# Q tiles scaled once and placed by small DMAs, sums normalised in their own buffers, a longer planned latency: a two-layer attention and MLP kernel on one core

## The chip, the core and the metric

The kernel runs on one core of one Trainium2 chip. Five engines of that core work side by side, each on its own queue of instructions and in the order of that queue: TensorE (PE, matrix products, written to PSUM), VectorE (DVE), ScalarE (ACT), GpSimd (POOL) and SyncE (SP). Here SP only starts DMA transfers, which sixteen DMA engines then carry out, and POOL starts some too. Engines wait for one another, and for DMAs, through semaphores. The metric is the device time of one execution in microseconds; a lower number is better.

## The reference

Two layers share their weights. Each layer is a self-attention block with 32 heads of 16 features and an MLP block with a ReLU. Both add to the residual stream `x` of 2048 rows and 512 columns (bf16), and both normalise their input without learned gains.

```python
def _A_ref(x, wqkv, wo):
    qkv = transpose((x @ wqkv).reshape(B, S, 3, H, Dh), 2, 0, 3, 1, 4)
    q, k, v = qkv[0], qkv[1], qkv[2]
    scores = einsum("bhqd,bhkd->bhqk", q, k) * (Dh ** -0.5)
    p = softmax(scores, axis=-1)
    o = einsum("bhqk,bhkd->bhqd", p, v)
    return transpose(o, 0, 2, 1, 3).reshape(B, S, D) @ wo
def _B_ref(x, w1, w2):
    return relu(x @ w1) @ w2

x = x + _A_ref(_layernorm(x), A_wqkv, A_wo)
x = x + _B_ref(_layernorm(x), B_w1, B_w2)
x = x + _A_ref(_layernorm(x), A_wqkv, A_wo)
x = x + _B_ref(_layernorm(x), B_w1, B_w2)
```

The costly part is the exponential: 32 heads x 2048 x 2048 scores in each layer.

## The kernel before

**Tiles.** The 2048 query rows are cut into chunks of 512 (the last two chunks of layer 1 are cut in halves of 256). A chunk is worked through in runs. A run is one T of four; T names 128 features of Q and K, that is eight heads. Within a T, a head is found by its group g (32 partitions each, four of them) and its parity e (which 16 of the 32). A run has two segments, one for each parity. A segment goes over blocks: 128 keys by 512 queries of one head.

**Slots.** The main loop forms slots of three blocks (W = 3). For each block PE makes the scores in one of two PSUM tiles `ps_s` of three banks (L1396), with a contraction over 32 partitions: 16 of the head and 16 of its neighbour, which must be zero in Q. ACT takes the exponential of the slot, out to `e` (L1405). In about half of the slots the third block goes to DVE instead, which makes its exponential from integer and half-precision steps on pairs of such blocks (`lin` L1090, then `step` and `cube` from L1131 on). ACT's instruction has then 1024 columns instead of 1536. PE multiplies the exponentials with the values, adding up in `ps_o` (L983). The values carry a column of ones, so that the sum of the exponentials comes out in a row of its own.

**Q.** `q_group` (L682) makes the Q tile of one run with sixteen matmuls into `ps_f` (L446). Its end, `fin`, lets DVE multiply the bank with two columns of a mask (L676): one read per parity, both written to `qbuf[n % 2]`, with the scale in the mask and zeros where the other parity stands. So DVE reads the bank twice in one instruction. The group for run n + 1 is put on the urgent list as soon as a block of run n is first taken.

**The end of a segment.** `finish_segment` (L867) copies `ps_o` to one of three buffers `u`, or, for segments whose first part was summed up earlier, adds the stored part to it and writes to `u` (L895, L897). SP then moves the row of sums to a compact tile `c` (L902), DVE takes the reciprocal (L924), SP puts it back (L925), and POOL spreads it over 32 partitions to one of three buffers `r` by a DMA (L927). For "quick" segments a DVE shuffle does the spreading instead (L937). At last DVE multiplies `u` with `r` into `ot` (L913), from which the output projection is made. A new segment's copy waits, through `run_until(("m", n - NU))`, until the product three segments earlier has been put in order.

**The rest.** Projections, layer norms and the MLP (`o_group`, `h_group`, `z_group`, K and V groups) are cut into pieces that fill PE between the slots. Weights of the MLP's first half come in tiles of 128 columns into four buffers `w1buf`; the load of tile n + 4 is issued by SP behind the matmuls of tile n (L714). Normalised rows are transposed by DMA from SP too (L571).

**What sets the order.** The order of instructions on each engine is written out by a planner that runs when the kernel is built. It keeps a clock for PE, DVE and ACT with fixed costs, marks when each result will be there (`mark`, with a planned lag for what comes by DMA: C_LAG for `c`, R_LAG for `r` by POOL, U_LAG for the quick ones), and puts an instruction in its queue when its inputs are due. On the chip nothing but the queues' order and the semaphores counts. One rule matters below: when the planner looks for a block for DVE, it may take one of a later run (FAR = 3 segments ahead), if that run's Q is marked at all:

```python
sg["l"] == mine["l"] and ahead.count(sg) + (sg is mine) > 1
and at([("q", sg["n"])], "pe") is not None
```

The pace of the filling work is `todo` divided by the slots that are left in the chunk, less or plus a constant.

Of the kernel before, what the change touches and what calls it, by code (L numbers as in the profile page):

```python
# [12 lines left out]
BF16 = mybir.dt.bfloat16  # L13
# [4 lines left out]
ALU = mybir.AluOpType  # L18
# [7 lines left out]
def kernel(  # L26
# [10 lines left out]
    nc = tc.nc  # L37
    P = 128
# [5 lines left out]
    DH = D // H  # L44
# [6 lines left out]
    QS = 512  # L51
    NQS = S // QS
    TPC = QS // P
    NT = 8
    SCALE = float(DH) ** -0.5
# [2 lines left out]
    NE = 5  # L58

    NACC = 8  # L60
    NW1 = 4
    NU = 3


# [2 lines left out]
    LOG2E = 1.4426950408889634  # L67
    UNIT = 128.0
# [8 lines left out]
    PE_TO_DVE, DVE_TO_PE, ACT_TO_PE, PE_TO_ACT = 220.0, 180.0, 240.0, 222.0  # L77
    DVE_TO_DVE, EVAC = 112.0, 612.0
    FLOOR = 0.56
    C_LAG, R_LAG, U_LAG = 3600.0, 10500.0, 3000.0  # L80
    VLAG = 1
    X_ISSUE, X_LAG = 1400.0, 7500.0
    RSTD_LAG = 4000.0
    AHEAD = (8.0, 8.0)
    LATE = 0.0
    MID = 2
# [15 lines left out]
    def sb(shape, dt, name):  # L102
        return persist.tile(shape, dt, name=name)
# [6 lines left out]
    wo = sb([P, NDC, D], BF16, "wo")  # L110
    w1buf = [sb([P, NDC, P], BF16, f"w1_{n}") for n in range(NW1)]
    w2 = sb([P, NF, D], BF16, "w2")
# [38 lines left out]
    acc0.append(kt1[:].bitcast(FP32).rearrange("p a b -> p (a b)"))  # L151
    ebuf = [sb([P, W * QS], BF16, f"e{n}") for n in range(NE)]
    qbuf = [sb([P, 2, QS], BF16, f"q{n}") for n in range(2)]
    ubuf = [sb([P, QS], FP32, f"u{n}") for n in range(NU)]
    rbuf = [sb([P, QS], FP32, f"r{n}") for n in range(NU)]
    cbuf = [sb([P, QS // 32], FP32, f"c{n}") for n in range(NU)]
# [38 lines left out]
    nc.sync.dma_start(out=w2[:], in_=B_w2[:, :].rearrange("(c p) f -> p c f", p=P))  # L195

    make_identity(nc, ident[:])
    for kb in range(NKB):
        nc.gpsimd.memset(vaug[0][kb][:, :, DH : DH + 2], 1.0)
    for kb in range(NKB - TPC):  # L200
# [47 lines left out]
    def mark(key, engine="dve", lag=0.0):  # L248
        made[key] = (engine, (now_pe if engine == "pe" else now_dve)[0] + lag)
# [135 lines left out]
    def finish_group():  # L385
        while cur:
            do_piece()
        while evac:
            do_evac()

    def run_until(key):

        if key in made:
            return
        finish_group()
        if key in made:
            return
        if key not in maker:
            kind, l, j = key[1]
            for i in range(chunks[l, j][1]):  # L400
                run_until(("z", l - 1, j, i) if kind == "ln1" else ("o", l, j, i))
        if key in made:
            return
        t = maker[key]
        for k in t["deps"]:
            run_until(k)
        if "pieces" in t:
            start_group(t)
            finish_group()
        else:  # L410
            do_task(t)
        assert key in made, key
# [51 lines left out]
    LAST = 5  # L464

    def columns(l, j):

        tt, n = chunks[l, j]
        return tt // TPC, tt % TPC * P, n * P
# [78 lines left out]
    def ln_rows(tag, tt, n, i):  # L548
# [10 lines left out]
        if i == n - 1:  # L559

            def rstd():
                ln_seed(tag, n)
                mark(("rs", tag, 3), lag=RSTD_LAG)

# [54 lines left out]
    def each(n, *key):  # L619
        return [key + (i,) for i in range(n)]  # L620
# [54 lines left out]
    def q_masked(n, b, w=QS):  # L675
        return nc.vector.tensor_mul(  # L676
            out=qbuf[n % 2][:, :, 0:w],
            in0=b.rearrange("p (e q) -> p e q", e=1).to_broadcast((P, 2, w)),
            in1=qmask.rearrange("p (e q) -> p e q", q=1).to_broadcast((P, 2, w)),
        )  # L680

    def q_group(n, l, j, T):  # L682
        xj, _, w = columns(l, j)
        cost = 90 + 2.09 * w

        def fin(b):
            q_masked(n, b, w)
            mark(("q", n))

        return mm_group(  # L690
            q_mms(l, j, T), fin, [("q", n)], each(TPC, "xnT", ("ln1", l, xj)), cost=cost,
            wide_by=w,
        )
# [16 lines left out]
    def load_w1(n):  # L710

        if n < len(chunks) * NF - NF + NW1:
            ft = n % NF
            nc.sync.dma_start(  # L714
                out=w1buf[n % NW1][:],
                in_=B_w1[:, ft * P : (ft + 1) * P].rearrange("(c p) f -> p c f", p=P),
# [5 lines left out]
    def h_group(l, j, ft, war):  # L722
# [19 lines left out]
        def after():  # L742
            for f in range(number):
                load_w1(n + f + NW1)
            if w1_to_load:
# [7 lines left out]
            [  # L753
                (w1buf[(n + f) % NW1][:, c, :], xnT[xj][:, c, a : a + w])
                for f in range(number) for c in range(NDC)
# [39 lines left out]
    def rest_of_chunk(l, j):  # L795

        if (l, j) == (1, LAST - 2):
            for ft in range(NF):
                home = (
                    w1buf[((l * NQS + LAST) * NF + ft) % NW1] if ft < NW1  # L800
                    else (kt01 + kt2)[(ft - NW1) // 2][:, ft % 2, :].rearrange(
# [61 lines left out]
    last_steps = []  # L863

    sums_wait = [0]

    def finish_segment(sg, last):  # L867
        l, j, t, e = sg["l"], sg["j"], sg["t"], sg["e"]
# [13 lines left out]
        n = norm_no[0]  # L882
        norm_no[0] += 1
        if n >= NU:
            run_until(("m", n - NU))
        u, r, c = ubuf[n % NU], rbuf[n % NU], cbuf[n % NU]
        lane = DH if e == 0 else DH - 1
        width = sg["w"]
        at_column = columns(l, j)[1]
# [1 line left out]
        c = c[:, 0 : width // 32]  # L891
# [17 lines left out]
        b = before(l, j)  # L909
# [258 lines left out]
    for e in range(2):  # L1168
        nc.vector.tensor_reduce(
            out=mask[e],  # L1170
            in_=ident[:].rearrange("p (g e d) -> p e g d", g=4, e=2)[:, e],
# [3 lines left out]
            out=qmask[:, e : e + 1], in0=mask[e], scalar1=SCALE * LOG2E * UNIT, scalar2=None,  # L1175
            op0=ALU.mult,
# [24 lines left out]
    b = plain(k_mms(0, 0))  # L1201
# [6 lines left out]
    b = plain(v_mms(0))  # L1208
# [58 lines left out]
    while units:  # L1267
# [6 lines left out]
        for (sg, kb, g), *_ in banked:  # L1274
            if sg["n"] not in seen:
                seen.add(sg["n"])
                n = sg["n"] + 1
# [12 lines left out]
        if len(banked) == W and pair_at in (None, no):  # L1290
# [3 lines left out]
            elif (not pairs or pair_no[0] + 1 - pairs[0]["n"] < NP) and ((mine['l'] or ("v", 0, 15) in made or len(pairs) < 3 and ("v", 0, 5) in made or not pairs and ("k", 0, 0, 1) in made) and (not mine['l'] or ('k', 1, 0, NQS - 1) in made or pace < PAIR_PACE)):  # L1294
# [7 lines left out]
                if now_dve[0] + waiting < now_pe[0] + BACKLOG:  # L1302
                    here = segs.index(mine)
                    first = max(here, segs.index(pairs[-1]["sg"])) if pairs else here
# [10 lines left out]
            if half is not None:  # L1315
# [22 lines left out]
                if far:  # L1338
                    units.remove(far)
                    units.appendleft(banked.pop())  # L1340
                    x = far
                elif fit or of_take:
                    x = fit or next((x for x in of_take[::-1] if x[0][2] not in other), of_take[-1])
                    banked.remove(x)
                else:
                    units.appendleft(banked.pop())
                    x = take_unit(heads(banked) + other, take)
# [13 lines left out]
        todo = left()  # L1361
        first = now[0][0]
        rest = to_come[first["l"], first["j"]] / W
        if first["l"] and first["early"]:
            rest = sum(x[0][0]["early"] for x in itertools.islice(units, 400)) / W - 20.0
        pace = (
            3.0 if first["short"] and not first["l"] else max(todo / max(rest + (-8.0 if first["j"] == NQS - 1 and not first["l"] else AHEAD[first["l"]] if first["j"] < (LAST if first["l"] else NQS - 1) else -6.0), 6.0), 0.5)
        )
        owed[0] = min(owed[0] + pace, 6.0) if todo else 0.0
        hurry[0] = pace > (  # L1370
# [15 lines left out]
        short = FLOOR * 1330.0 - level - busy[0] - MM * (1 + soon)  # L1386
        times = 1 + min(spare, max(0, math.ceil(short / MM)))
        b = ps_s[no % 2][:].rearrange("p w q -> p (w q)")
# [13 lines left out]
        m = len(now) - len(taken)  # L1402
        while len(pend) == NE:
            force_v()
        ex = nc.scalar.activation(  # L1405
            out=eb[:, 0 : place[m]], in_=b[:, 0 : place[m]], func=ACTF.Exp,
# [33 lines left out]
    l, j = 1, LAST  # L1440
# [60 lines left out]
    for ft in range(NF + 1):  # L1501
        if ft < NF:
            b = more[ft % 4]
# [5 lines left out]
            if ft % 2:  # L1509
                out = nc.scalar.activation(out=ht[ft][:, at_column : at_column + width], in_=at_bank(b)[:, 0:width], func=ACTF.Relu)  # L1510
            else:
                out = nc.vector.tensor_scalar(
                    out=ht[ft][:, at_column : at_column + width], in0=at_bank(b)[:, 0:width],
                    scalar1=0.0, scalar2=None, op0=ALU.max,
                )
# [7 lines left out]
    for i in rows:  # L1523
# [3 lines left out]
            out=out_flat[(tt + i) * P : (tt + i + 1) * P, :], in_=x_t[tt + i][:]  # L1527
# [31 lines left out]
```

The softmax here doesn't subtract the row's maximum and nothing guards it: scores larger than these inputs give would overflow.

## Time and profile before

| | |
|---|---|
| median of 3 runs | 1589.63 us (1586.18 to 1590.61) |
| the profiled execution | 1588.44 us, of which 1586.6 us from its first to its last instruction |
| TensorE clock granted | 0.995 |
| exponentials on ACT | 1366, of them 702 with 1024 columns |
| Q evacuations on DVE | 52, the first by itself in the start |
| DMAs issued by SP | 353, of them 24 transposes |
| POOL's spreads r<-u | 59; 7.3 us (256 KB) and 4.9 us (128 KB) from issue to landing |

A row of the groups reads: line, engine, operation, what is written and read with shapes, count; then busy time in us and mean duration in ns; then the engine's idle time just before these instructions and what ended most of it. A row of the timeline reads: start and length in us, engine (a q behind it means its queue, which only issues), line, operation, tiles, count, and in brackets the idle time before with its releaser. An instruction's duration contains pipelining with its neighbours: exponentials overlap by some 0.1 to 0.25 us, and DVE instructions by some 0.1.

### The profile page before, as it was taken

The page shows a single profiled execution, that of the slowest core. Times are in us where ns is not written, and L with a number is a line of the kernel's source. Part 1 is how long each engine was busy: PE and PEld are TensorE (multiplying, and loading weights), DVE is VectorE, ACT ScalarE, POOL GpSimd, SP SyncE. Part 2 cuts the span into 40 slices and gives each one's busy share as a digit, 9 for nine tenths or more (in the row PEclk, how much of TensorE's full clock was granted, in tenths as well). Part 3 has the DMA queues.
Part 4 walks back from the last instruction along what each step waited for, and adds up shares of the span by engine and source line. Part 5 has one row for each costly group of instructions (what it writes and reads, how often), then busy time and mean ns, then how long its engine had stood idle before and what let it go on. Part 6 is the DMA issues. An engine that isn't in the chain of part 4 may idle for free.

```text
span 1586.6 us, 45174 instructions
## 1 busy us (share of the span) xinstructions
PE 1430.4 (90%) x19752; PEld 536.9 (34%) x19752; DVE 1506.7 (95%) x2910; ACT 1545.3 (97%) x1383; POOL 101.3 (6%) x240
## 2 busy tenths in 40 slices
PE   8888889998899989999899998888999999999898
PEld 3222223222233322322223222223334444544454
DVE  7899999999999999999899998899999999999994
ACT  7999999999999999999999999999999999999994
POOL 2000001001010010100100001001001000010100
PEclk9999999999999999999999999999999999999998
DMA  6001101111012120120101000000210111313030
GB/s 193 15 2 26 18 9 22 39 25 25 6 19 45 23 29 7 25 48 13 26 2 28 21 2 1 2 4 9 54 25 16 40 33 27 74 26 80 13 62 15
DMA packets 128885, 45.57 MB, mean 29 GB/s; under 512 B 117840, under 2 KB 125776, under 8 KB 128688
## 3 DMA queue, kind: packets, MB, share of 16 engines
q1 hardware_dynamic: 114752, 29.36, 8.6%
q0 software_dynamic: 12592, 12.02, 4.3%
q8 instruction: 154, 2.52, 0.7%
q10 hardware_dynamic: 1344, 1.31, 0.2%
q14 instruction: 43, 0.35, 0.1%
HBM read 24.38 MB, written 2.10 MB: 17 GB/s over the span
## 4 chain that ended last, share of the span: by engine, by line
ACT 81%; PE 8%; DVE 7%; issue 2%; DMA 1%; ACTq 0%; DVEq 0%
ACT e L1405 81%; PE ps_s L1396 3%; PE ps_f L446 2%; DVE lin L1090 2%; PE ps_o L983 2%; DVE step L1131 1%; PE ps_s L1458 1%; DVE cube L1146 1%; DVE cube L1142 1%; DMA wqkv<-in_A_wqkv_dram 1%; DMA r<-u 0%; DVE ht L736 0%; DVE q L676 0%; DVE ot L913 0%; DVE stats L481 0%
## 5 line engine op out<-in xcount | busy, mean ns | idle before, releaser
L1405 ACT ACTIVATE e<-ps_s 128x1536 bf16<-128x1536 f32 (+1 forms) x1366 | 1536.7, 1362 | 8.5 <-PE ps_s L1396 8.1
L1396 PE MATMUL ps_s<-q,ktp 32*128 32x512 bf16 (+1 forms) x6136 | 608.1, 341 | 112.4 <-ACT e L1405 99.2
L983 PE MATMUL ps_o<-e,vaug 128*32 128x512 bf16 (+1 forms) x4236 | 500.8, 346 | 14.1 <-DVE u L897 8.3
L1090 DVE TENSOR_SCALAR lin<-ps_s 128x512 int16<-128x512 f32 x702 | 478.3, 685 | 24.5 <-PE ps_s L1396 18.1
L1396 PEld LDWEIGHTS <-ktp 32*128 32x128 bf16 x6136 | 200.3, 92 | 563.6 <-issue 418.9
L1131 DVE TENSOR_SCALAR step<-lin 128x1024 int16<-128x1024 int16 x702 | 275.3, 419 | 1.9 <-PE ps_o L983 0.9
L983 PEld LDWEIGHTS <-vaug 128*32 128x32 bf16 x6052 | 173.8, 95 | 300.9 <-issue 282.2
L1142 DVE TENSOR_TENSOR cube<-step 128x1024 f16<-128x1024 bf16 x351 | 238.4, 683 | 1.6 <-PE ps_o L983 0.2
L1146 DVE TENSOR_TENSOR cube<-cube,lin 128x1024 bf16<-128x1024 f16 x351 | 238.0, 679 | 0.0
L446 PE MATMUL ps_f<-w,ht 128*32 128x512 bf16 x1624 | 151.6, 381 | 1.8 <-DVE x L768 0.5
L446 PE MATMUL ps_f<-xnT,w 128*32 128x512 bf16 (+1 forms) x2016 | 146.3, 345 | 5.8 <-DVE ht L736 3.6
L983 PE MATMUL ps_o<-step,vaug 128*32 128x512 bf16 (+1 forms) x884 | 151.0, 340 | 0.0
L983 PE MATMUL ps_o<-cube,vthird 128*32 128x512 bf16 (+1 forms) x836 | 148.9, 339 | 0.0
L983 PE MATMUL ps_o<-lin,vaug 128*32 128x512 bf16 (+1 forms) x884 | 125.9, 339 | 4.6 <-DVE u L897 3.2
L927 POOL DMA_DIRECT2D r<-u x59 | 43.1, 731 | 1168.6 <-DVE lin L1090 341.7
L446 PE MATMUL ps_f<-xnT,wqkv 128*32 128x512 bf16 (+1 forms) x1312 | 109.4, 365 | 6.2 <-DVE ktp L626 1.1
L446 PE MATMUL ps_f<-wo,ot 128*32 128x512 bf16 x960 | 90.3, 381 | 1.2 <-DVE x L700 1.2
L736 DVE TENSOR_SCALAR ht<-ps_f 128x512 bf16<-128x512 f32 x105 | 72.0, 685 | 2.3 <-PE ps_f L446 1.5
L446 PEld LDWEIGHTS <-w 128*32 128x32 bf16 x2016 | 57.5, 96 | 33.9 <-issue 18.7
L676 DVE TENSOR_TENSOR q<-ps_f,masks 128x1024 bf16<-128x1024 f32 (+1 forms) x51 | 53.6, 1052 | 9.1 <-PE ps_f L446 8.1
L446 PEld LDWEIGHTS <-ht 128*32 128x32 bf16 x1624 | 46.9, 96 | 25.3 <-issue 11.9
L983 PEld LDWEIGHTS <-vthird 128*32 128x32 bf16 x836 | 43.6, 95 | 33.5 <-issue 28.7
(103 smaller groups left out, 609.4 us busy)
## 6 DMA issues: line engine op xcount, KB each, us to landing
w<-in_B_w_dram SPq DMA_DIRECT2D x130, 128.0 KB
r<-u POOLq DMA_DIRECT2D x32, 256.0 KB, 7.3
r<-u POOLq DMA_DIRECT2D x27, 128.0 KB, 4.9
out_dram<-x SPq DMA_DIRECT2D x16, 128.0 KB
x<-in_A_x_dram SPq DMA_DIRECT2D x14, 128.0 KB
w<-in_B_w_dram SPq DMA_DIRECT2D x1, 1792.0 KB
ktp<-in_B_w_dram SPq DMA_DIRECT2D x10, 128.0 KB
wqkv<-in_A_wqkv_dram ACTq DMA_DIRECT2D x2, 512.0 KB
```

Of the source, the lines that this page charges most:

```text
L446: nc.tensor.matmul(out[cols], lhsT[:, cols], rhs, start=i % k == 0, stop=i % k == k - 1, tile_position=(0, 32 * g), skip_group_check=True,)
L676: return nc.vector.tensor_mul(out=qbuf[n % 2][:, :, 0:w], in0=b.rearrange("p (e q) -> p e q", e=1).to_broadcast((P, 2, w)), in1=qmask.rear ...
L736: nc.vector.tensor_scalar(out=out, in0=sums, scalar1=0.0, scalar2=None, op0=ALU.max)
L927: nc.gpsimd.dma_start(out=r[:, 0:width], in_=bass.AP(tensor=sums.tensor, offset=sums.offset, ap=[list(sums.ap[0]), [0, 32], [1, width]],),)
L983: nc.tensor.matmul(ps_o[32 * g : 32 * g + 32, 0 : sg["w"]], values[:, 4 * sg["T"] + g, 2 * e : 2 * e + 32], rhs, start=g not in sg["begun" ...
L1090: first = nc.vector.tensor_scalar(out=lin[which][:, half * QS : (half + 1) * QS], in0=src, scalar1=EXP_BIAS, scalar2=0.0, op0=ALU.add, op1 ...
L1131: nc.vector.tensor_scalar(out=stair, in0=line, scalar1=keep, scalar2=put, op0=ALU.bitwise_and, op1=ALU.bitwise_or,)
L1142: (609, lambda: nc.vector.tensor_mul(out=power, in0=mantissa, in1=mantissa)),
L1146: (609, lambda: nc.vector.tensor_mul(out=power.bitcast(BF16), in0=power, in1=line.bitcast(BF16))),
L1396: nc.tensor.matmul(b[:, a : a + sg["w"]], kt[32 * g : 32 * g + 32, kc : kc + P], qbuf[sg["n"] % 2][32 * g : 32 * g + 32, sg["e"], 0 : sg[" ...
L1405: ex = nc.scalar.activation(out=eb[:, 0 : place[m]], in_=b[:, 0 : place[m]], func=ACTF.Exp, scale=1.0 / (LOG2E * UNIT),)
L1458: uses(nc.tensor.matmul(out, lhsT, rhs, start=first, stop=last), b, needs=needs)
```

## The change

There are four edits, made together.

1. Q: DVE reads the bank once, scales it, and writes bf16 to one new tile `qraw`. Eight DMAs from SP then copy the sixteen rows of each group and parity to their place in `qbuf`, whose other rows were filled with zeros once, by POOL, in the start. The mark of Q has a planned lag Q_LAG of 6 us. `qraw` is a single buffer.
2. Sums: a segment with a stored first part adds `ps_o` into that stored buffer, and the DMAs and the product work on it there. `u` and `r` come from one ring of the six buffers; a buffer is waited for only when it is taken from the ring. The compact tile `c` is waited for by ("r", n - NU).
3. R_LAG goes from 10.5 to 13 us.
4. NW1, the number of w1 buffers, goes from 4 to 3, and the constant in the pace of the last chunk from -6 to -11.

```diff
-    NW1 = 4
+    NW1 = 3
...
-    C_LAG, R_LAG, U_LAG = 3600.0, 10500.0, 3000.0
+    C_LAG, R_LAG, U_LAG = 3600.0, 13000.0, 3000.0
...
+    Q_LAG = 6000.0
...
+    qraw = sb([P, QS], BF16, "qraw")
...
+    for q in qbuf:
+        nc.gpsimd.memset(q[:], 0.0)
...
     def q_group(n, l, j, T):
         xj, _, w = columns(l, j)
-        cost = 90 + 2.09 * w
+        cost = 77 + 1.045 * w
 
         def fin(b):
-            q_masked(n, b, w)
-            mark(("q", n))
+            nc.vector.tensor_scalar(
+                out=qraw[:, 0:w], in0=b, scalar1=SCALE * LOG2E * UNIT, scalar2=None, op0=ALU.mult
+            )
+            for e in range(2):
+                for a in range(16 * e, P, 32):
+                    nc.sync.dma_start(
+                        out=qbuf[n % 2][a : a + DH, e, 0:w], in_=qraw[a : a + DH, 0:w]
+                    )
+            mark(("q", n), lag=Q_LAG)
...
+    ring = deque((x, None) for us in zip(ubuf, rbuf) for x in us)
...
         if n >= NU:
-            run_until(("m", n - NU))
-        u, r, c = ubuf[n % NU], rbuf[n % NU], cbuf[n % NU]
+            run_until(("r", n - NU))
+        c = cbuf[n % NU]
+
+        def room():
+            buf, of = ring.popleft()
+            if of is not None:
+                run_until(("m", of))
+            ring.append((buf, n))
+            return buf
+
+        u = room() if sg["load"] is None else sg["load"]
+        r = room()
...
-            3.0 if first["short"] and not first["l"] else max(todo / max(rest + (-8.0 if first["j"] == NQS - 1 and not first["l"] else AHEAD[first["l"]] if first["j"] < (LAST if first["l"] else NQS - 1) else -6.0), 6.0), 0.5)
+            3.0 if first["short"] and not first["l"] else max(todo / max(rest + (-8.0 if first["j"] == NQS - 1 and not first["l"] else AHEAD[first["l"]] if first["j"] < (LAST if first["l"] else NQS - 1) else -11.0), 6.0), 0.5)
```

The very first Q tile is still made by the old way in the start.

## The prediction

> **What bounds the kernel now.** I read the busy shares and the chain that ended last, then ACT's groups by shape, then the idle time in front of ACT's exponentials, and last the DMA queue of SP around the Q tiles and around the longest ACT gap.
>
> ```profile
> PE 1430.4 (90%) x19752; PEld 536.9 (34%) x19752; DVE 1506.7 (95%) x2910; ACT 1545.3 (97%) x1383; POOL 101.3 (6%) x240
> ...
> ACT 81%; PE 8%; DVE 7%; issue 2%; DMA 1%; ACTq 0%; DVEq 0%
> ```
> ```profile
> L1405 ACT ACTIVATE e<-ps_s 128x1536 bf16<-128x1536 f32 x663 | 1005.1, 1578 | 4.8 <-PE ps_s L1396 4.4 <-PE ps_o L983 0.3
> L1405 ACT ACTIVATE e<-ps_s 128x1024 bf16<-128x1024 f32 x702 | 760.8, 1159 | 3.6 <-PE ps_s L1396 3.6
> L676 DVE TENSOR_TENSOR q<-ps_f,masks 128x1024 bf16<-128x1024 f32 x35 | 42.7, 1220 | 8.8 <-PE ps_f L446 8.1 <-PE ps_s L1396 0.3
> L676 DVE TENSOR_TENSOR q<-ps_f,masks 128x512 bf16<-128x512 f32 x16 | 10.9, 684 | 0.4 <-PE ps_s L1396 0.3
> L1090 DVE TENSOR_SCALAR lin<-ps_s 128x512 int16<-128x512 f32 x702 | 478.3, 685 | 24.5 <-PE ps_s L1396 18.1
> ```
>
> ACT sets the time: from its first exponential at 14.4 us to its last at 1557.6 it is busy 1536.7 of 1543.2 us. So an edit pays in two ways only: fewer columns for ACT, or less of those 6.5 us; and every new ACT gap is paid in full. DVE, at 95%, matters by the gaps that it makes on ACT. Two places show how such gaps come about. The first is the DMA chain u, c, u, r at 384 us (SP's, POOL's, DVE's, PE's and ACT's rows, in order of time):
>
> ```profile
> 384.41 6.28 SPq L571 DMA_TRANSPOSE xnT<-xn  x4
> ...
> 390.86 0.56 SPq L925 DMA_DIRECT2D u<-c  x1
> ...
> 393.25 0.79 POOL L927 DMA_DIRECT2D r<-u  x1 [10.26 <-DVE step L1131]
> ...
> 400.58 0.75 DVE L913 SCALAR_TENSOR_TENSOR ot<-u,masks,r 128x512 bf16<-128x512 f32 x1 [2.55 <-DMA r<-u]
> ...
> 402.43 1.94 ACT L1405 ACTIVATE e<-ps_s 128x1024 bf16<-128x1024 f32 x2 [1.71 <-PE ps_s L1396]
> ...
> 407.32 1.02 ACT L1405 ACTIVATE e<-ps_s 128x1024 bf16<-128x1024 f32 x1 [1.35 <-PE ps_s L1396]
> ```
>
> Four transposes hold SP, the small DMA behind them goes out 5 us late, DVE waits 2.55 us for the spread, ACT loses 1.71 + 1.35 = 3.06 us. A DVE wait goes through to ACT. The second is a Q tile that is needed at once:
>
> ```profile
> 60.57 1.22 DVE L676 TENSOR_TENSOR q<-ps_f,masks 128x1024 bf16<-128x1024 f32 x1
> ...
> 61.84 0.37 PE L1396 MATMUL ps_s<-q,ktp 32*128 32x512 bf16 x1 [0.26 <-DVE q L676]
> ...
> 63.56 1.45 ACT L1405 ACTIVATE e<-ps_s 128x1536 bf16<-128x1536 f32 x1 [0.16 <-PE ps_s L1396]
> ```
>
> PE was ready at 61.19 (two matmuls of the same slot start there), the third waited for Q until 61.84, and ACT lost 0.16: of 0.65 us of delay, 0.49 is cushion.
>
> **What the Trainium skill says.** "DMA: Bandwidth & Descriptors", section on the anatomy of one DMA: a fixed cost of some 2 us, most of it the receipt of the write. The trace agrees from below: SP's wait list has
>
> ```profile
> SPq L925 <- DMA c<-u: 66.5, 52, 4.0
> ```
>
> so after issuing c<-u (0.56 us, median of 78) SP waits 66.5/52 = 1.28 us more until it has landed: 1.8 us from issue to landing. The same page, section on issuing engines, says that issuing from several engines saves only sequencer time; here SP alone issues, so that is what the change spends. "VectorE: DVE Perf Modes", errata section, prices a PSUM source at 120 cycles plus one per element at 0.96 GHz: 0.66 us for 512 columns, 1.19 for 1024; the rows above show 0.685 and 1.22. So halving the columns read does nearly halve the instruction.
>
> **The change part by part.**
>
> *Q's evacuation.* 35 instructions of 1.220 and 16 of 0.684 (53.6 us) become 35 of 0.685 (the price of lin, same shape and source) and 16 of 0.42 (u<-ps_o, 128x256: 417 ns): 30.7 us. DVE saves 22.9 us. The planner spends it: the built order has 355 DVE pairs for 351, each 2 x 0.685 + 2 x 0.419 + 0.683 + 0.679 = 3.57 us, 14.3 in all. DVE stays some 9 us lighter. Eight more exponentials are 1024 wide instead of 1536, at 1578 - 1159 = 419 ns each: **-3.4 us** on ACT.
>
> *Eight DMAs for each Q tile.* 51 x 8 = 408 issues more on SP, which had 353. None is shown before; nearest rows: 0.37 us (w1 loads), 0.56 (c<-u), and 0.06 for the wait in front. I take 0.45 for one, 3.6 for a batch; bounds 0.37 and 0.60. Landing 1.8 us after issue (bounds 1.6 and 2.3). Each matmul of before waits for one evacuation; in the built order of after it waits for just the piece of its row group and head parity. Most tiles stand 8 to 40 slots (about 1.13 us each) ahead of use: hidden. But the planner pulls one block of the next run forward for DVE as soon as Q is marked, whatever the mark's time, so the new Q_LAG moves nothing there. In seven tiles (5, 29, 30, 31, 32, 35, 36, counting the first as 0) that block stands one slot behind the evacuation, and the exponential of its slot waits for it. With evacuation start E, piece 0 is there at E + 0.69 + 0.07 + 1.8 + 0.05 = E + 2.6, piece 1 at E + 3.05. Against first use in the trace of before (E, use): 29: 1008.76, 1010.34, piece 1, 1.47 late; 30: 1022.15, 1023.41, piece 1, 1.79; 31: 1033.87, 1035.14, 1.33; 32: 1046.95, 1048.21, 1.34; 35: 1151.16, 1152.77, 0.99; 36 (256 wide, E + 2.34): 1161.65, 1163.15, 0.84; tile 5, whose place is new: as the worst, 1.8. Sum 9.6, less 7 x 0.49 cushion: **+6.2 us** (3 to 10).
>
> *What stands behind a batch on SP.* c<-u behind it lands up to 3.6 us late, and recip (L924), then all of DVE, waits. In after's DVE order most of them have 3.7 us or more of work between copy and recip; four have too little (short by 0.5 to 1.6 us, 3.9 in all; work is counted there without the idle time between, so I take half): **+2** (0 to 6). u<-c of the quick segments is directly behind a batch in tiles 30 to 33; DVE's shuffle is then up to 1 us short, partly covered by the same stall of Q: **+1** (0 to 4). The first tiles: batch 1 waits for the landing of the first w1 loads (25.9 us), the four transposes behind it move from 23.4 to about 26.4, land by 34, and are read at 37.7: 0 (to 3).
>
> *R_LAG 10.5 to 13.* Moves each product 2.5 us back in DVE's order; the 2.55 us wait at 400 us goes: **-2.9** (-3.1 to 0). What is late next there is nothing: ACT is full again.
>
> *Sums in their own buffers, three w1 buffers, -11 for -6.* The same adds write another tile: 0, and the freed buffers take away forced order, not work. Loads of w1 stand at least 4 slots (4.5 us) ahead of use in after's order, against 0.37 + 2 us of landing: +0.5 (0 to 3). The last chunk is paced earlier: fewer matmuls of values stand behind the last exponential (22 and 4 of another kind, for 30): **-0.5**. DVE's 9 us of slack: -1 (-3 to 0) of the 3 us in small ACT gaps elsewhere. POOL's two fills of Q lie in its idle start.
>
> Sum: -3.4 + 6.2 + 2 + 1 - 2.9 + 0.5 - 0.5 - 1 = +1.9. On the profiled execution's 1588.4 (span 1586.6 and 1.8 around it) that is 1590.3; the median of the runs shown is 1589.6, 1.2 higher, so 1591.5; I say **1591**.
>
> **The rivals.** *No change (the forecast)*: gains and new stalls cancel, 1585 to 1594.
>
> *Faster*: the pieces land sooner (0.37 and 1.6: piece 0 at E + 2.35) and the lighter DVE evacuates earlier, so the seven stalls shrink to some 2 us and nothing waits on SP: -3.4 - 2.9 - 0.5 - 1 + 2 = -5.8, 1583. For it: no ACT gap stands at tiles 29 to 36 now. Against: in 29 to 32 DVE starts within 0.1 us of PE's end, so E cannot come earlier.
>
> *Slower*: SP's queue becomes what DVE waits for. One mechanism: a batch holds SP; a copy of sums typically ends 2 us behind Q's evacuation, and its recip stands 3.7 us of DVE work behind it, of which the landing needs 1.9. So a batch longer than 2 + 1.8 = 3.8 us, 0.48 an issue, makes DVE wait. At 0.6 us an issue it is 4.8 us, and each of some twelve copies (26 in after's order follow a batch within 4.5 us) waits 1 us: 12 us, and the seven stalls cost 8.5: -7.8 + 12 + 8.5 = +13, 1604. For it: the place at 384 us, where SP held for 6 us cost ACT 3. Against: SP's large loads go at 0.37.
>
> *The change doesn't do what it says*, for Q_LAG: it is so at the pulled blocks, and is in the forecast.
>
> **How the numbers follow.** About 0.3% (4.8 us) is what a measurement can tell from no change. No change 0.40, slower 0.38, faster 0.22; the slower case is given more than its sum since the bounds of the unknown costs reach further up than down. The range takes in the faster case's 1583 with its lower bounds (-5) and the slower one's 1604 with 3 more: 1578 to 1607, leaving some 0.2. The likeliest case's own range is 1585 to 1594.
>
> **What would show it.** Q's evacuations at 0.685 and 0.42; eight Q issues of about 0.45 on SP; ACT's 1024 form 710 times; ACT gaps of about 1 us, seven of them, ended by PE's scores that wait for DMA q<-qraw; no wait for r<-u at 400 us. Wrong if DVE idles for c or r by more than 3 us in all, if batches take over 4.5 us, or if pieces land later than 2.3 us after issue.

## The result, and the profile after

The changed kernel takes 1674.26 us (median of four runs, 1668.23 to 1676.28) against 1588.74 us for the kernel before beside it: a ratio of 1.0533, 95% interval 1.0501 to 1.0565. It is slower by some 85 us, far outside the predicted range.

The page of the kernel after, its busy shares, the granted clock in 40 slices and the chain that ended last:

```profile
span 1671.5 us, 46102 instructions
...
PE 1486.8 (89%) x19757; PEld 533.0 (32%) x19757; DVE 1496.8 (90%) x2933; ACT 1554.9 (93%) x1383; POOL 103.3 (6%) x242
...
PEclk9999999999999999999979999799989999799999
...
ACT 50%; PE 21%; DVE 20%; DMA 5%; issue 2%; SPq 1%; DVEq 0%; ACTq 0%
```

ACT held 81% of the chain before and holds 50% now; PE has 21% and DVE 20%. And the clock row, which had 9 everywhere but in its last slice, has dips to 7. The groups of the kernel after by shape, for the exponentials and for Q's evacuation:

```profile
L1427 ACT ACTIVATE e<-ps_s 128x1536 bf16<-128x1536 f32 x655 | 976.2, 1540 | 40.4 <-PE ps_s L1418 38.7 <-PE ps_o L1005 0.3
L1427 ACT ACTIVATE e<-ps_s 128x1024 bf16<-128x1024 f32 x710 | 749.3, 1118 | 44.9 <-PE ps_s L1418 43.7
...
L691 DVE TENSOR_SCALAR qraw<-ps_f 128x512 bf16<-128x512 f32 x35 | 24.0, 685 | 9.0 <-PE ps_f L450 6.0 <-DMA xnT<-xn 2.8
L691 DVE TENSOR_SCALAR qraw<-ps_f 128x256 bf16<-128x256 f32 x16 | 6.7, 418 | 0.1
```

The counts and durations are the predicted ones: 710 exponentials of 1024 columns, evacuations of 685 and 418 ns. What is new is the third figure of the first two rows: ACT was idle 4.8 + 3.6 us before them, now 40.4 + 44.9.

These gaps make up the loss. From the starts of the exponentials in the trace: before, 14 of them were followed by a gap; now 130 are. One followed at once by the next takes 0.92 us (1024) or 1.34 us (1536) from start to start, one with a gap behind it 1.64 or 2.20 us. That is 72 x (1.635 - 0.917) + 58 x (2.196 - 1.338) = 101 us above the pace without gaps, for 9 us before. The difference of 92, less 8 x 0.42 for the narrower exponentials, is 89; the end of the last exponential moved from 1557.6 to 1644.2 us, by 86.6. (The gaps by themselves are 83.3 us; the rest is overlap of neighbouring exponentials that a gap takes away.)

The list of waits of the kernel after (engine, tile and line that waited, what for; us in all, times, longest) says what ends them:

```profile
ACT e L1427 <- PE ps_s L1418: 82.3, 95, 3.5
...
DVE c L946 <- DMA c<-u: 28.6, 13, 4.5
...
PE ps_s L1418 <- DMA q<-qraw: 13.9, 8, 2.9
...
PE ps_f L450 <- DMA w<-in_B_w_dram: 10.1, 6, 3.3
```

ACT waits for PE's scores. Behind PE stand three kinds of late DMA, all from SP's queue. The first and the last made nothing wait in the kernel before, and the second did not exist: the sums on their way to the reciprocal (38.4 us of DVE's time with the two smaller rows for `c`, 9.5 more for quick spreads), Q itself (13.9) and w1 (10.1). One place where all three queue up, from the timeline of SP, DVE, PE and ACT in the kernel after:

```profile
1440.09 5.96 SPq L696 DMA_DIRECT2D q<-qraw  x8
...
1443.20 0.41 DVE L919 COPY u<-ps_o 128x256 f32<-128x256 f32 x1
...
1446.14 1.09 SPq L725 DMA_DIRECT2D w<-in_B_w_dram  x2
1447.33 0.61 SPq L924 DMA_DIRECT2D c<-u  x1
...
1449.27 0.20 DVE L946 RECIPROCAL c<-c 128x8 f32<-128x8 f32 x1 [1.81 <-DMA c<-u]
...
1450.09 0.40 PE L450 MATMUL ps_f<-xnT,w 128*32 128x256 bf16 x4 [2.88 <-DMA w<-in_B_w_dram]
...
1451.08 1.45 ACT L1427 ACTIVATE e<-ps_s 128x1536 bf16<-128x1536 f32 x1 [3.19 <-PE ps_s L1418]
```

A batch of eight Q copies holds SP for 5.96 us. Two loads of w1 and the copy of sums go out behind it; PE idles 2.88 us for the first, DVE 1.81 us for the second, and ACT 3.19 us for PE. The sums had been ready since 1443.61, when DVE's copy to `u` ended; their own copy went out 3.7 us later.

All 51 batches take from 4.93 to 9.27 us, median 5.55. An issue has a median of 0.559 us, and 0.092 us lie between two. In some batches pieces wait longer, as they overwrite a Q tile that PE is still reading: SP's own wait list for the kernel after has

```profile
SPq L696 <- PE ps_s L1418: 54.2, 111, 2.1
```

The second half of the story is in the clock. A Q tile that comes late, in the timeline of the kernel after:

```profile
1036.69 0.69 DVE L691 TENSOR_SCALAR qraw<-ps_f 128x512 bf16<-128x512 f32 x1
...
1037.40 5.79 SPq L696 DMA_DIRECT2D q<-qraw  x8
...
1040.63 1.01 PE L1418 MATMUL ps_s<-q,ktp 32*128 32x512 bf16 x4 [2.07 <-DMA q<-qraw]
...
1041.67 1.02 ACT L1427 ACTIVATE e<-ps_s 128x1024 bf16<-128x1024 f32 x1 [2.21 <-PE ps_s L1418]
...
1043.20 2.56 ACT L1427 ACTIVATE e<-ps_s 128x1536 bf16<-128x1536 f32 x2 [0.50 <-PE ps_s L1418]
```

PE waits 2.07 us for the pieces, ACT 2.21; and after Q is there, ACT waits again. The same place in windows of 3.41 us (busy time and instructions of PE, PEld, DVE, ACT and POOL, then granted clock, DMA share, GB/s):

```profile
1033.16:1036.57 3.41, 3.03 (x38) 0.83 (x30) 3.37 (x7) 3.41 (x4) 0.00 (x0) 1.00 0.00 0
1036.57:1039.99 3.42, 1.18 (x13) 0.46 (x10) 1.70 (x4) 2.89 (x3) 0.00 (x0) 1.00 0.04 10
1039.99:1043.40 3.41, 2.77 (x16) 0.48 (x17) 0.69 (x1) 1.23 (x2) 0.00 (x0) 0.50 0.12 28
1043.40:1046.81 3.41, 3.17 (x22) 0.56 (x17) 2.36 (x5) 2.92 (x3) 0.00 (x0) 0.50 0.04 8
1046.81:1050.23 3.42, 3.42 (x27) 0.78 (x24) 1.62 (x5) 2.04 (x3) 0.00 (x0) 0.50 0.00 0
1050.23:1053.64 3.41, 2.86 (x34) 0.91 (x30) 3.38 (x8) 3.41 (x3) 0.00 (x0) 1.00 0.03 5
```

In the second window PE was busy for only 1.18 us. In the three that follow it has half its clock: it is busy nearly all the time with fewer matmuls, and ACT gets 1.23, 2.92 and 2.04 us of work. The clock returns after a window in which PE was busy throughout. In the whole run the clock is halved for 142 us (17 before; some 2 us of each figure lie behind the last instruction), and 38.0 of ACT's 83.3 us of gaps lie in those stretches.

### The profile page after: what moved, and what is told of

It is laid out like the page before. It is cut to its first block, busy times and chain, and to the rows that moved or that the text cites. A ratio compares the mean times of both kernels' runs of the same rounds, so it can differ in the third digit from the quotient of the medians.

```text
span 1671.5 us, 46102 instructions
## 1 busy us (share of the span) xinstructions
PE 1486.8 (89%) x19757; PEld 533.0 (32%) x19757; DVE 1496.8 (90%) x2933; ACT 1554.9 (93%) x1383; POOL 103.3 (6%) x242
## 4 chain that ended last, share of the span: by engine, by line
ACT 50%; PE 21%; DVE 20%; DMA 5%; issue 2%; SPq 1%; DVEq 0%; ACTq 0%
ACT e L1427 50%; PE ps_s L1418 7%; PE ps_o L1005 6%; PE ps_f L450 6%; DVE lin L1112 5%; DVE step L1153 3%; DVE cube L1168 2%; DVE cube L1164 2%; DMA c<-u 1%; DMA q<-qraw 1%; DVE ht L747 1%; DMA w<-in_B_w_dram 1%; PE ps_s L1480 1%; DVE ot L935 1%; DVE qraw L691 1%
## 5 line engine op out<-in xcount | busy, mean ns | idle before, releaser
L1427 ACT ACTIVATE e<-ps_s 128x1024 bf16<-128x1024 f32 (+1 forms) x1366 | 1546.2, 1320 | 85.4 <-PE ps_s L1418 82.3
L1418 PE MATMUL ps_s<-q,ktp 32*128 32x512 bf16 (+1 forms) x6125 | 629.8, 353 | 113.1 <-ACT e L1427 78.5
L1112 DVE TENSOR_SCALAR lin<-ps_s 128x512 int16<-128x512 f32 x710 | 483.9, 685 | 62.1 <-PE ps_s L1418 57.3
L1005 PE MATMUL ps_o<-e,vaug 128*32 128x512 bf16 (+1 forms) x4228 | 512.4, 356 | 13.5 <-DVE u L919 8.1
L1418 PEld LDWEIGHTS <-ktp 32*128 32x128 bf16 x6125 | 193.5, 93 | 591.4 <-issue 416.1
L450 PE MATMUL ps_f<-xnT,w 128*32 128x512 bf16 (+1 forms) x2016 | 156.0, 354 | 19.6 <-DMA w<-in_B_w_dram 10.1
L1005 PE MATMUL ps_o<-step,vaug 128*32 128x512 bf16 (+1 forms) x892 | 156.0, 350 | 8.7 <-DVE step L1153 8.7
L1005 PE MATMUL ps_o<-lin,vaug 128*32 128x512 bf16 (+1 forms) x892 | 132.9, 345 | 4.2 <-DVE u L919 2.2
L949 POOL DMA_DIRECT2D r<-u x52 | 38.6, 742 | 1057.8 <-DVE step L1153 323.2
L946 DVE RECIPROCAL c<-c 128x16 f32<-128x16 f32 (+1 forms) x78 | 17.7, 226 | 38.3 <-DMA c<-u 28.6
```

What stands on the lines that cost most here:

```text
L450: nc.tensor.matmul(out[cols], lhsT[:, cols], rhs, start=i % k == 0, stop=i % k == k - 1, tile_position=(0, 32 * g), skip_group_check=True,)
L946: nc.vector.reciprocal(out=c, in_=c)
L949: nc.gpsimd.dma_start(out=r[:, 0:width], in_=bass.AP(tensor=sums.tensor, offset=sums.offset, ap=[list(sums.ap[0]), [0, 32], [1, width]],),)
L1005: nc.tensor.matmul(ps_o[32 * g : 32 * g + 32, 0 : sg["w"]], values[:, 4 * sg["T"] + g, 2 * e : 2 * e + 32], rhs, start=g not in sg["begun" ...
L1112: first = nc.vector.tensor_scalar(out=lin[which][:, half * QS : (half + 1) * QS], in0=src, scalar1=EXP_BIAS, scalar2=0.0, op0=ALU.add, op1 ...
L1418: nc.tensor.matmul(b[:, a : a + sg["w"]], kt[32 * g : 32 * g + 32, kc : kc + P], qbuf[sg["n"] % 2][32 * g : 32 * g + 32, sg["e"], 0 : sg[" ...
```

## The experiments

Theory A, formed from these views: the batches hold SP's queue; what stands behind them, and Q itself, comes late; and a PE stall costs more than its own length, since half the clock follows. The rivals: B, the third w1 buffer is what is missing; C, the planner's other order (pace, latency, own buffers); D, it is the Q pieces' landing, whoever issues them; E, the clock has no part.

All runs in one table, the waits from each profile in us: of DVE for sums (for the reciprocal and for quick spreads), of PE's scores for Q, of PE for w1, of DVE's layer norm for POOL; then the time at half clock.

| kernel | ratio to before (95%) | sums | Q | w1 | POOL | half clock |
|---|---|---|---|---|---|---|
| before | 1 | 0 | 0 | 0 | 0 | 17 |
| after | 1.0533 (1.0501-1.0565) | 38.4 + 9.5 | 13.9 | 10.1 | 0.2 | 142 |
| q_masked_back | 1.0028 (1.0011-1.0046) | 0 | 0 | 1.8 | 0 | 25 |
| q_dma_alone | 1.0458 (1.0437-1.0479) | 34.7 + 10.0 | 15.4 | 6.0 | 0 | 110 |
| nw1_alone | 1.0037 (1.0025-1.0050) | 0 | 0 | 1.7 | 0 | 20 |
| q_pool_queue | 1.0221 (1.0198-1.0245) | 1.6 | 16.9 | 0.5 | 8.3 | 82 |
| rest_alone | 0.9986 (0.9966-1.0005) | 0 | 0 | 0 | 0 | 29 |
| q_pool_inplace | 1.0281 (1.0259-1.0304) | 0.8 | 25.1 | 0 | 3.5 | 82 |
| stalls_long | 1.0262 (1.0237-1.0287) | 0 | 0 | 0 | 0 | 64 |
| stalls_short | 1.0072 (1.0054-1.0091) | 0 | 0 | 0 | 0 | 45 |
| q_due | 1.0610 (1.0588-1.0633) | 48.5 + 23.5 | 0.6 | 8.1 | 7.3 | 117 |
| q_due_pool | 1.0167 (1.0150-1.0185) | 2.3 | 0 | 1.4 | 13.2 | 49 |
| q_due_inplace | 1.0152 (1.0124-1.0179) | 1.4 | 0 | 0 | 8.1 | 38 |
| sums_pool | 1.0286 (1.0255-1.0317) | 5.7 + 0.2 | 14.0 | 10.1 | 0 | 72 |
| q_due_sums_pool | 1.0209 (1.0188-1.0230) | 11.0 + 1.5 | 0 | 6.8 | 3.3 | 60 |
| old_pace | 1.0525 (1.0482-1.0569) | 45.2 + 8.8 | 14.3 | 9.5 | 0 | 127 |
| old_lag | 1.0417 (1.0376-1.0458) | 33.3 + 2.7 | 15.0 | 0.5 | 0 | 113 |

### Which part of the change is it?

*q_masked_back*: the changed kernel, only Q as before.

```diff
-        cost = 77 + 1.045 * w
+        cost = 90 + 2.09 * w
 
         def fin(b):
-            nc.vector.tensor_scalar(
-                out=qraw[:, 0:w], in0=b, scalar1=SCALE * LOG2E * UNIT, scalar2=None, op0=ALU.mult
-            )
-            for e in range(2):
-                for a in range(16 * e, P, 32):
-                    nc.sync.dma_start(
-                        out=qbuf[n % 2][a : a + DH, e, 0:w], in_=qraw[a : a + DH, 0:w]
-                    )
-            mark(("q", n), lag=Q_LAG)
+            q_masked(n, b, w)
+            mark(("q", n))
```

> The changed kernel with the two masked DVE reads of PSUM put back in place of the Q copies; three w1 buffers, the longer spread latency, own buffers and the new pace stay. Theory A (each batch of eight Q copies holds SP's queue for 5 to 8 us; the sums and w1 loads behind it and the Q pieces themselves come late; every PE stall of a microsecond or more is followed by half the TensorE clock for 3.4 us or more): 1580 to 1592 us, reciprocal's waits for DMA under 3 us, no more than five stretches of half clock. Rival B (the third w1 buffer is what is missing): 1605 us or more, PE still waits some 20 us for w. Rival C (the planner's other order, pace and ring): over 1640 us.

Measured: 1595.3 us. The copies are 79 of the 85 us, and the reciprocal waits for nothing. Rivals B and C fall as main causes; the 1595 is 3 above the range given for theory A.

*q_dma_alone*: the kernel before with the Q copies (`fin` of the change, `qraw`, the fill of `qbuf`) and `NW1 = 3`.

> The kernel before with the Q copies alone (and the third w1 buffer gone, for their room). Theory A: 1660 to 1690 us, with 12 to 22 stretches of half clock, as the whole change. Rival C: below 1620 us.

Measured: 1662.4 us, with 15 stretches of half clock in the loop. The copies, with the w1 buffer given up, reproduce the loss but for 12 us; on those, old_lag below.

*nw1_alone*: `-    NW1 = 4` / `+    NW1 = 3` in the kernel before.

> The kernel before with three w1 buffers in place of four, nothing else. Theory A: 1586 to 1593 us, PE waits less than 2 us for w in all. Rival B: 1600 us or more, PE waits for w 15 us or more.

Measured: 1595.8 us, about 6 more than before, though PE's wait for w1 is only 1.7 us. Theory A's number was too low, rival B's too high. That one wait stands in the tail. From the timeline of this run, two of PE's rows after the last exponential, which ends at 1560.7:

```profile
...
1564.13 0.62 PE L446 MATMUL ps_f<-xnT,w 128*32 128x256 bf16 x16 [1.73 <-DMA w<-in_B_w_dram]
1564.58 3.19 PE L446 MATMUL ps_s<-w,ht 128*32 128x512 bf16 x56
```

Work of the MLP that the kernel before had done between the slots (its PE has no row of L446 after the last exponential) is left over; that three buffers let fewer tiles start ahead is the likely reason, not a measured one. From the last exponential to the end it takes 33.6 us, for 29.0 before; the last exponential itself ends 3.1 us later. `qraw` is as large as the w1 buffer that the change gives up, so this can be counted as a price of the copies as well. It accounts for q_masked_back's 1595.3: with the fourth buffer back and `qraw` left out, that kernel is rest_alone, the next one.

*rest_alone*: the changed kernel with the masked reads, without `qraw` and with `NW1 = 4`: the spread latency, own buffers and pace by themselves.

> The change without its Q copies and with all four w1 buffers: the masked DVE reads of PSUM, the longer spread latency, the own buffers and the new pace. The prediction's terms for these parts: the stall near 400 us gone (-2.9) and the last chunk's pace (-0.5), so 1585 to 1587 us; rival: what goes there comes back elsewhere, 1588 to 1592 us, with as much ACT idle as before (6.5 us between exps).

Measured: 1587.85 us beside 1588.82; the interval of the ratio holds 1. The stall near 400 us is gone, and about as much idle time stands elsewhere (8.7 us of gaps between exponentials). This is the best of all these versions, and no measurable gain.

### SP's queue, or the pieces' landing?

*q_pool_queue*: `nc.gpsimd.dma_start` for `nc.sync.dma_start` in the Q copies. *sums_pool*: the same replacement for the two small copies of the sums (`c<-u`, `u<-c`), Q staying on SP.

> The changed kernel with the Q copies issued by POOL, so that SP's queue holds none of them. Theory A with SP's queue as the larger part: reciprocal's waits fall from 38 to under 8 us and PE's waits for w from 22 to under 5; the waits for Q stay near 14 to 30 us, as POOL needs some 0.74 us an issue by the row of r<-u; 1600 to 1645 us. Rival D (it is the landing of the Q pieces that costs, whoever issues them): Q waits over 40 us and 1660 us or more. Rival B: the waits for w stay at 20 us.

> The changed kernel with the sums' two small copies (to c and back) issued by POOL, so that they no longer stand behind Q's batches; Q, w1 and the transposes stay on SP. Theory A: the reciprocal's waits for DMA fall from 38 to under 10 us, PE's waits for Q and w stay at 14 and 22 us, and the time is 1635 to 1660 us. Rival (it is DVE's order, not SP's queue, that makes the reciprocal wait): its waits stay above 25 us and the time at 1665 us or more.

Measured: 1624.5 and 1633.2 us. In q_pool_queue the waits for sums and for w1 are gone though there are still three w1 buffers, so w1 too was late because of the queue. Its list of waits:

```profile
PE ps_s L1418 <- DMA q<-qraw: 16.9, 7, 8.3
...
DVE c L946 <- DMA c<-ht: 1.6, 1, 1.6
...
PE ps_f L450 <- DMA w<-in_B_w_dram: 0.5, 1, 0.5
```

And that of sums_pool:

```profile
PE ps_s L1418 <- DMA q<-qraw: 14.0, 9, 3.1
...
PE ps_f L450 <- DMA w<-in_B_w_dram: 10.1, 6, 2.6
...
DVE c L946 <- DMA c<-u: 3.1, 4, 1.1
```

Taking the copies off SP saves 50 us, taking only the sums off SP 41 us (1633.2 is 2 us below the range given). The two overlap and are not to be added. Rival D, 1660 us or more, falls: a piece lands as late when POOL issues it (1.72 us after its issue, median, for 1.78 from SP), and landing is the smaller part.

*q_due*: the copies on SP again, but in the built order no Q tile is read sooner than 4 slots after its evacuation (seven were after one). *q_due_pool* is the same with the copies issued by POOL, *q_due_sums_pool* with the sums' copies on POOL instead.

```diff
-                            and at([("q", sg["n"])], "pe") is not None
+                            and (at([("q", sg["n"])], "pe") or 1e9) < now_pe[0]
...
         run_dve(exp_end[no - 1] + ACT_TO_PE, musts)
+        for g in list(urgent):
+            if not cur and at(g["deps"], "pe") is not None:
+                run_until(g["makes"][0])
```

> The changed kernel, its copies still on SP, with the planner told to start a Q tile's group as soon as its inputs are there, and to take a tile for DVE's blocks only when its planned time is past: no tile is then read sooner than 4 slots after its evacuation (in the changed kernel seven are after one slot). Theory A (SP's queue is the larger part, the pieces' landing the smaller): PE's waits for Q fall from 14 to under 4 us, the reciprocal's waits for DMA stay above 20 us and PE's for w above 10, and the time is 1635 to 1660 us. Rival D (the landing is the larger part): 1620 us or less.

> The same planner's order and the copies issued by POOL. Theory A: nothing is left of the loss but the third w1 buffer's 6 us: 1590 to 1603 us, PE's waits for Q and the reciprocal's for DMA under 4 us each, half clock in no more than six stretches. If POOL's own work (the spread and the layer norm's small operations behind a batch) takes the place, DVE waits for POOL and it is 1605 to 1625 us.

> Q copies on SP with the planner's order that reads Q later, and the sums' small copies on POOL. Theory A with parts that add up: no waits for Q and under 6 us of the reciprocal's for DMA; what is left is w1 behind the batches (PE waits 10 to 20 us) and the third buffer: 1600 to 1618 us. Rival (reading Q later costs by its own order of work, as its 1684.6 us suggests): 1630 us or more.

Measured: 1684.6, 1615.0 and 1622.8 us. In q_due the waits for Q are gone, and it is slower still, where 1635 to 1660 had been expected:

```profile
DVE c L946 <- DMA c<-u: 35.8, 18, 4.2
...
DVE r L959 <- DMA ktp<-c: 8.9, 2, 5.1
...
PE ps_s L1418 <- DMA q<-qraw: 0.6, 1, 0.6
```

The batches now fall in other places, and more sums stand behind one: 72 us of DVE's waits for 48. So with the queue held, giving Q more time bought nothing. With the queue free, it bought 10 us (1624.5 to 1615.0), less than expected: the batches on POOL hold something else. In the timeline of q_due_pool:

```profile
761.45 0.49 POOL L696 DMA_DIRECT2D q<-qraw  x1 [2.21 <-PE ps_s L1418]
...
764.03 1.04 POOL L502 TENSOR_TENSOR ya<-va,masks 128x4 f32<-128x4 f32 x1
...
765.10 0.41 DVE L532 TENSOR_SCALAR xn<-x,mv,ya 128x512 bf16<-128x512 bf16 x1 [4.88 <-POOL ya L502]
```

The last piece of a batch waits 2.21 us for PE to finish reading the old tile; the layer norm's small operations stand behind it on POOL, and DVE waits 4.88 us for their result. q_due_sums_pool is 5 us above its range: w1 stands behind the batches still, and DVE waited 4.6 us for one copy of sums.

*q_pool_inplace*: no copies at all. DVE writes Q unmasked to `qbuf`, POOL multiplies it with the two masks there; four w1 buffers. *q_due_inplace*: the same with the order of q_due.

```diff
+            q = qbuf[n % 2]
+            nc.vector.tensor_copy(out=q[:, 0, 0:w], in_=b)
+            for e in (1, 0):
+                nc.gpsimd.tensor_scalar(
+                    out=q[:, e, 0:w], in0=q[:, 0, 0:w], scalar1=qmask[:, e : e + 1], scalar2=None,
+                    op0=ALU.mult,
+                )
...
```

> The change with Q still read from PSUM once, by a copy of 685 ns to 418 ns, but put in place by two POOL multiplications with the mask in SBUF and no copy by DMA; four w1 buffers. Theory A (the copies on SP and their landing are the whole loss): at most 1592 us, no wait of the reciprocal for DMA over 3 us in all. If two POOL multiplications of 512 columns take over 1.5 us each, PE waits for POOL at the seven tiles that are used one slot later, and the time is 1595 to 1610 us.

> Q read from PSUM once, masked by two POOL multiplications (1.56 us each as measured), four w1 buffers, and the planner's order that reads a tile later. Theory A: with the Q waits gone 1582 to 1592 us, and the eight shorter exps worth up to 3.4 us. If POOL's work takes the place: 1600 us or more, with DVE waiting for POOL.

Measured: 1634.5 and 1612.1 us. The first is far above both of its ranges; the second is what was expected if POOL's work takes the place. POOL takes 1.75 us for a multiplication of 512 columns and 1.13 for one of 256 (1.56 is the mean of all 102); the pulled blocks wait 25.1 us for it in the first, and in the second the layer norm waits 8.1 us for POOL. So leaving out the DMAs for Q is not enough: a longer way to the tile costs 46 us while seven tiles are read one slot after their evacuation, and the later order takes half of that away (q_due_inplace). The 23 us that are left there are explained by the wait for POOL only in part; the rest was not sought.

### What the clock adds

*stalls_long* and *stalls_short*: the kernel before, with DVE work added that the planner doesn't know of, 48 statistics instructions in all: 12 times four in a row, or 48 times one. Their results are read by nobody.

```diff
...
+        if no % 90 == 20 and 190 < no < 1280:
+            for i in range(4):
+                nc.vector.bn_stats(out=warm[:, 1:], in_=w2[:, i, :])
```

> The kernel before with 12 unplanned DVE stalls spread over the loop: four statistics instructions in a row (about 2.75 us by their row of 0.69 us each) whose result nobody reads. Theory A (a PE stall of a microsecond or more brings half the clock in the next windows): ten or more new stretches of half clock, about a third of ACT's new gaps inside them, and 30 to 45 us more. Rival E (a stall costs only what DVE's slack does not cover): no new stretches of half clock, 12 x (2.75 - 1) = 21 us or less.

> The same DVE work as in 12 stalls of four instructions, now as 48 single ones of about 0.69 us. Theory A: each is too short to empty PE for a microsecond, so no more than three new stretches of half clock and at most 10 us more. Rival E: the same sum of DVE work costs about the same as in twelve stalls, 15 us or more.

Measured: 1630.0 and 1601.0 us. The same DVE work costs 41 us in twelve pieces and 12 us in 48. A stall of 2.88 us costs 41.1 / 12 = 3.4 us, more than its own length. The clock is halved in 13 stretches of the loop (3 before), and 19.1 of 44.2 us of ACT's gaps lie in them. In stalls_short there are eight such stretches, more than I had allowed for, and 12 us is above the 10 expected; still it falls far from rival E, which has the two cost the same, and stalls_long is about double what rival E gave it.

The contrast of long and short does not show the clock's part by itself, since a short stall can also vanish in the cushion between DVE and ACT. The gaps tell them apart: of the 37.7 us by which stalls_long has more of them than the kernel before, 20.8 lie at full clock, about the 21 of rival E's sum, and 16.9 at half clock. This is an account by place; no run changes the clock and nothing else. Windows of stalls_long around a stall of DVE that began at 660.66:

```profile
662.09:665.50 3.41, 1.32 (x17) 0.43 (x17) 3.35 (x5) 1.18 (x2) 0.00 (x0) 1.00 0.03 6
665.50:668.91 3.41, 3.41 (x24) 1.07 (x25) 2.87 (x6) 2.64 (x3) 0.00 (x0) 0.50 0.01 1
668.91:672.33 3.42, 3.42 (x25) 0.82 (x20) 2.55 (x6) 2.75 (x3) 0.27 (x1) 0.50 0.02 2
672.33:675.74 3.41, 3.41 (x42) 1.22 (x41) 3.07 (x6) 3.19 (x4) 0.51 (x1) 1.00 0.21 35
```

The same picture without any Q copy: a window with PE busy for 1.32 us, then two at half clock in which ACT gets 2.6 to 2.8 us of work.

### The 12 us between the copies alone and the whole change

*old_pace*: `-11.0` back to `-6.0`. *old_lag*: `R_LAG` back from 13000 to 10500; each in the changed kernel.

> The changed kernel with the old pace of the last chunk (-6 for -11). If the pace is what costs beside the copies: 1658 to 1666 us. If it is another part: 1668 to 1682 us.

> The changed kernel with the old planned latency of the spread (10500 for 13000). If the latency is what costs beside the copies: 1658 to 1666 us. If it is another part: 1668 to 1682 us. If both kernels stay above 1668, the own buffers and their ring are left.

Measured: 1674.2 and 1655.6 us, the second 2 us below its range. The pace does nothing; the longer planned latency costs 19 us beside the copies, while it costs nothing measurable without them (rest_alone). That is more than the 12 us in question: old_lag is 7 us faster than q_dma_alone, so the own buffers may give something back, but the intervals of these two runs overlap. By the waits, w1 loads no longer meet the batches with the old latency (0.5 us for 10.1), and sums less often. It is a matter of which transfers come to stand behind a batch; why just this order does was not followed further.

## Why the prediction was wrong

*Q's evacuation*: counts and durations came out as predicted (710, 685 and 418 ns). That ACT gains 3.4 us by it is in the sum of the result section, but no run has it alone.

*Eight DMAs for each Q tile*: the mechanism and the places were right: PE waits for Q at just the seven tiles named, twice at tile 36, for 13.9 us in all where 9.6 were predicted; 2.94 of them are the second wait at tile 36, whose batch took 9.27 us. The landing was right too, 1.78 us from issue (median; predicted 1.8). That figure rested on the trace; the section quoted beside it in the prediction describes DMAs issued by GpSimd, and these were SP's. The issue was mis-sized: 0.559 us and 0.092 between two, not 0.45 with all included; a batch takes 5.55 us (median), not 3.6, and every one is beyond the 4.5 named as refuting. The price had been taken between the 0.37 of w1 loads and the 0.56 of c<-u, where the nearer kin, a small copy from SBUF to SBUF, was the second alone.

*What stands behind a batch on SP* is the step that failed: +2 and +1 predicted, 48 us of DVE waits measured, and 41 us of time when only the sums leave SP's queue (sums_pool). With a cover of 3.7 us of DVE work, a hold of 3.6 looked harmless and one of 5.55 is not: up to a threshold the DVE work covers it, and beyond it most copies behind a batch become a DVE stall. In the trace of after 29 of the 78 copies of sums to `c` go out within 4.5 us of a batch's end; the reciprocal waits for 17 of these, and for none of the other 49. The sum had set a middle value for a cost that lies on one side of such a threshold or on the other; the prediction's own slower rival had put it at 3.8 us a batch. Besides, the prediction took a batch for eight issues in a row; pieces also wait for PE to release the old tile, and the whole queue with them. The transposes of the first tiles, set at 0, were late for DVE by up to 2.8 us, and ACT has no gap over 0.5 us there.

*Three w1 buffers*: "at least 4 slots (4.5 us) ahead of use" counted the time from a free queue. Behind a batch of 5.55 us that lead is gone: 10.1 us of PE waits, which vanish with the copies off SP. And the buffer alone costs 6 us (nw1_alone), where +0.5 was set, mostly because MLP work is left for the tail; the prediction only asked whether loads come in time.

*What no step had* is the clock. All stalls were priced at their length, less the cushion. The trace of before had a case: the 2.55 us wait near 400 us was followed by half clock from 403.9 to 407.3 us, and the second gap quoted there, 1.35 us at 407.32, lies at the end of that stretch. It was read as part of the same wait. How much of the 85 us is due to the clock no run isolates; 35.8 of ACT's 76.8 us of new gaps lie at half clock. The loop also repeats score matmuls where its own count of PE's work in a slot falls short of `FLOOR` x 1330 ns, which helps nothing in a wait that the planner doesn't foresee.

*R_LAG, own buffers, pace, DVE's slack*: the wait at 400 us went, but rest_alone has no measurable gain of the -2.9, -0.5 and -1, and with the copies the longer latency costs 19 us.

*The rival on the slower side* named the right mechanism, SP's queue becoming what DVE waits for, and gave it 0.38. Its 0.6 us an issue was nearly right (0.65 with what lies between). Its price fell short: it counted twelve copies at 1 us, left out w1 and the waits inside a batch, and had no clock. So 1604 came out in place of 1674.

## What to carry to other kernels

Before moving work to small DMAs, add up how long one burst holds the queue that issues it, and compare that with the lead of everything else on that queue; where the lead is shorter, count a full stall for most of them, not a middle value. Price a stall of PE by what the clock does afterwards, not by its length. A buffer given up can cost at the end of the program though nothing ever waits for it in the loop.

## What the runs showed of the hardware

The Trainium skill ("TensorE: Matmul & The Clock Gate", Part 1 on the clock gate) describes a free-running window of 3413 ns after which TensorE's clock goes to half when idle, and back to full after a busy one; its section on oscillation warns of PE gaps above some 3.4 us. The traces agree on the window: every stretch of half clock in the loop lasts a multiple of 3.41 us, and within each run all begin at the same phase of such windows. They differ on the gap: in the loop of the kernel after PE's longest pause is 3.32 us, and there are 19 stretches of half clock. I cut the loops (first exponential to last) of the kernels before and after and of the fifteen others into these windows. Of windows at full clock with PE busy for less than half of the time, all 81 were followed by half clock; between 0.5 and 0.7, 82 of 228; at 0.7 or more, 7 of 7224. At half clock, full clock came back after 165 of 242 windows with PE busy for 0.95 or more, and after 3 of 81 below that. The longest pause of PE inside the 170 windows ahead of half clock has a median of 1.4 us. So in this kernel a PE stall of 1 to 2 us, well placed, is enough, and it takes a nearly fully busy window to get back. Busy time here is that of the profile, in which some matmul records may be missing.

The other page, "DMA: Bandwidth & Descriptors", says that issuing from several engines saves only the sequencer's time, "usually small relative to the DMA itself". The landing, 1.72 us for 1.78, fits the first half. But in this kernel that time was the larger part of the loss: the same 408 copies took 4.12 us a batch (median) from POOL and 5.55 from SP, and moving them saved 50 us, as nothing on SP then stood behind them.
